# Performer attention and channel mixer on one core: the first channel product of three chunks by Strassen, in a re-ordered list

## Chip, cores and metric

One NeuronCore of a Trainium2 chip runs the whole kernel. The metric is the device time of one execution in microseconds (us). Engines: PE (TensorE, matmuls; weight loads run beside them as PEld), DVE (VectorE), ACT (ScalarE), POOL (GpSimd), SP (SyncE, which here only issues DMAs).

## What is computed

Linear attention with exponential features (8 batches, 8 heads, 576 rows of 64, 128 features), then a mixer over tokens and over channels with weights `w_tok1` 576x256, `w_tok2` 256x576, `w_ch1` 512x1536 and `w_ch2` 1536x512. Inputs and output are float32; the kernel multiplies in float16.

```python
def phi(x):
    proj = np.einsum('bhsd,md->bhsm', x, omega)
    sq = np.sum(x * x, axis=-1, keepdims=True) / 2.0
    h = proj - sq
    return np.exp(h - np.max(h, axis=-1, keepdims=True)) / np.sqrt(m)
kv = np.einsum('bhsm,bhsd->bhmd', k_p, v)
num = np.einsum('bhsm,bhmd->bhsd', q_p, kv)
den = np.einsum('bhsm,bhm->bhs', q_p, k_p.sum(2))[..., None] + 1e-06
x = (num / den).transpose(0, 2, 1, 3).reshape(8, 576, 512)
u = x + (np.maximum(x.transpose(0, 2, 1) @ w_tok1, 0) @ w_tok2).transpose(0, 2, 1)
out = u + np.maximum(u @ w_ch1, 0) @ w_ch2
```

## The kernel before, in words

Rows 0 to 511 of a batch form a chunk (c = 0 to 7, one for each batch). The 64 last rows of all eight batches together form a ninth, the tail chunk (c = 8). For each batch `attention` (L522) makes the features of k and q (matmuls L657, L669; exponentials on ACT, L515), sums them over rows (L681), scales v by the inverse (`vs_`, L687, mostly on POOL), and forms kv (L702, L709) and the normalised output (L735, L737, read by DVE at L744 and L745). `token_mix` (L765) makes the token products (L771, L778, L791), adds x (`uadd`, L794), and has u transposed by a DMA of SP's queue into uT. The tail rows go through L845, L851 and `tail_transpose` (L855).

`channel_mix` (L956) then makes, for one chunk, the first channel product: 12 blocks of 128 hidden channels, each 4 matmuls of 128x512 (L967) into one PSUM bank. A relu on ACT or DVE (L290, L292) reads each bank into r3, in float16. The second channel product (`channel_out_fast`, L858) is already done by Strassen's scheme with 7 products of 2x2 blocks in place of 8: four sums of weight blocks (T, L448, once), four sums of r3 blocks for a chunk, each in two instructions of 128x768 (S and r, L295 by DVE), 7 products of 12 matmuls of 128x256 (L917), in the order X, Y, X, Z, X, Z, X of the banks that they accumulate in, and reads of the banks by DVE (L906) that add u and the parts. The tail chunk does its seven products in halves. Then the rows are stored (L946, L953, L1011). Only chunk 0 does a plain second product (L1001).

Nothing of the order is found at run time. A `Planner` (L121) holds jobs: an engine, the jobs it depends on, the ring slots that it takes and gives back. `ORDER` (L22) is a list of job numbers, kept in the file; each engine issues its own jobs in that order, and a job that waits holds up everything behind it on its engine. A negative number in ORDER is a warm-up matmul in the bank of that number. `SLOT` (L83) says which slot of its ring (or which PSUM bank, 8 in all) each tile gets, and `MOVED` (L93) puts a job on another engine than its usual one.

Of the kernel before, what the change touches and what calls it, by code (L numbers as in the profile page):

```python
# [9 lines left out]
FP32 = mybir.dt.float32  # L10
FP16 = mybir.dt.float16
AF = mybir.ActivationFunctionType
ALU = mybir.AluOpType
# [93 lines left out]
def key_of(name, b):  # L107

    return NEAR.get(str(b), {}).get(name, KEYS[name])


class Job:
    def __init__(self, eng, cost, key, fn, deps, take, give, rows, wire):
# [958 lines left out]
```

## Time and profile before

| | |
|---|---|
| three runs | 282.96, 283.94, 285.21 us |
| median | 283.94 us |
| span of the profiled execution (first to last instruction on the core) | 281.1 us |
| what the median has around that span | 2.84 us |
| mean granted clock of PE while busy, as shares of full speed | 1.00 |
| bytes read from and written to HBM | 35.95 MB, 16.52 MB |

The profiled execution has no time of its own beside its span; the 2.84 us are the difference between the two rows above them. A row of a group of instructions gives line, engine, operation, tiles out and in, shapes and count; then busy us and mean ns of one; then the idle time ahead of them and what ended it. A row of a timeline gives start and length in us, engine, line and tiles; in brackets stands the idle time before it and what released it. A row of the chain gives start, length, engine, what is written, line and count.

### The profile page before, as it was taken

The numbers are of one execution on the slowest core, as the hardware profiler recorded it, in microseconds if no ns is written. First come the engines' busy times: TensorE is split into PE (matmuls) and PEld (weight loads), VectorE is DVE, ScalarE is ACT, GpSimd is POOL, SyncE is SP. The second block draws the span as 40 slices with busy tenths as digits, with TensorE's granted clock in tenths as the row PEclk, the third lists the DMA queues.
The fourth block names the chain that finished last, engine by engine and source line by source line (L and its number), as shares of the span: only waits on it lengthen the run. The fifth ranks groups of instructions, "written<-read, shape, count | busy, mean of one in ns | idle before, by whom it ended". The sixth has DMA issues, their size and how long they took to land.

```text
span 281.1 us, 6278 instructions
## 1 busy us (share of the span) xinstructions
PE 270.3 (96%) x2526; PEld 167.6 (60%) x2526; DVE 222.4 (79%) x462; ACT 138.6 (49%) x288; POOL 92.0 (33%) x116
## 2 busy tenths in 40 slices
PE   6899999999999999999999999999999999999993
PEld 2547546443657755665667647755676467446782
DVE  2589828499999899996997999977995893565992
ACT  1498994049676418743758445734753510031200
POOL 8574994007510872048008710510033000000001
PEclk9999999999999999999999999999999999999999
DMA  6999999999998999997979993960151304030125
GB/s 161 194 189 161 157 169 213 178 191 202 179 218 184 148 172 186 181 198 104 212 178 185 241 135 101 161 156 2 76 97 59 111 0 96 0 149 2 75 90 135
DMA packets 80524, 39.66 MB, mean 141 GB/s; under 512 B 63984, under 2 KB 76016, under 8 KB 80304
## 3 DMA queue, kind: packets, MB, share of 16 engines
q0 software_dynamic: 31744, 17.74, 44.1%
q1 hardware_dynamic: 46832, 15.77, 29.1%
q10 hardware_dynamic: 1920, 5.77, 5.4%
q8 instruction: 19, 0.31, 0.4%
q14 instruction: 9, 0.07, 0.1%
HBM read 35.95 MB, written 16.52 MB: 187 GB/s over the span
## 4 chain that ended last, share of the span: by engine, by line
PE 89%; DVE 3%; DMA 2%; ACT 2%; issue 0%; SPq 0%; DVEq 0%
PE bank L967 32%; PE bank L917 26%; PE bank L791 5%; PE bank L778 5%; PE bank L1001 4%; PE bank L735 3%; PE bank L657 3%; PE bank L702 3%; DMA wc<-in_k_dram 2%; PE bank L669 2%; ACT kp L515 1%; PE bank L845 1%; PE bank L817 1%; PE bank L737 1%; PE bank L771 1%; DVE T L448 1%
## 5 line engine op out<-in xcount | busy, mean ns | idle before, releaser
L967 PE MATMUL bank<-uT,wc 128*128 128x512 f16 x376 | 89.6, 379 | 0.5 <-DVE r L292 0.4
L290 ACT ACTIVATE r<-bank 128x512 f16<-128x512 f32 (+1 forms) x86 | 47.7, 601 | 82.7 <-PE bank L967 61.5
L295 POOL TENSOR_TENSOR vs<-v,vs 128x512 f16<-128x512 f16 x32 | 34.2, 1072 | 94.4 <-DVE vs L683 51.3
L967 PEld LDWEIGHTS <-wc 128*128 128x128 f16 x424 | 38.8, 98 | 38.8 <-issue 1.6
L917 PEld LDWEIGHTS <-r 128*128 128x128 f16 x384 | 36.8, 98 | 8.2 <-issue 1.1
L515 ACT ACTIVATE kp<-bank 128x512 f16<-128x512 f32 x64 | 36.7, 618 | 8.9 <-PE bank L657 7.1
L515 ACT ACTIVATE qp<-bank 128x512 f16<-128x512 f32 x64 | 36.7, 614 | 8.8 <-PE bank L669 5.8
L681 DVE TENSOR_REDUCE km<-kp 128x8 f16<-128x1024 f16 x32 | 38.7, 1208 | 1.2 <-ACT kp L515 1.1
L292 DVE TENSOR_SCALAR r<-bank 128x512 f16<-128x512 f32 (+1 forms) x40 | 26.3, 670 | 15.7 <-PE bank L967 11.3
L745 DVE TENSOR_TENSOR x<-bank,rc 128x320 f16<-128x320 f32 x62 | 30.5, 492 | 2.1
L917 PEld LDWEIGHTS <-S 128*128 128x128 f16 x288 | 28.1, 98 | 5.8 <-issue 0.3
L906 DVE TENSOR_TENSOR o<-u,bank 128x512 f32<-128x512 f16 x28 | 19.0, 679 | 6.2 <-PE bank L917 5.8
L917 PE MATMUL bank<-T,r 128*128 128x256 f16 x192 | 23.8, 273 | 0.0
L917 PE MATMUL bank<-wc,r 128*128 128x256 f16 x192 | 23.6, 273 | 0.0
L917 PE MATMUL bank<-T,S 128*128 128x256 f16 x192 | 23.4, 273 | 0.0
L946 POOL DMA_DIRECT2D out_dram<-o x2 | 1.3, 645 | 61.2 <-issue 61.2
L906 DVE TENSOR_TENSOR o<-o,bank 128x512 f32<-128x512 f32 (+1 forms) x27 | 16.6, 617 | 2.5 <-PE bank L917 1.8
L735 PEld LDWEIGHTS <-qp 128*128 128x128 f16 x256 | 13.5, 98 | 8.1 <-DVE kvsb L286 0.7
L794 DVE TENSOR_TENSOR u<-x,bank 128x512 f16<-128x512 f16 x28 | 17.6, 680 | 0.0
L735 PE MATMUL bank<-kvsb,qp 128*128 128x65 f16 x256 | 15.0, 193 | 0.5 <-DVE kvsb L286 0.5
L791 PE MATMUL bank<-r,w 128*128 128x512 f16 x56 | 14.1, 381 | 0.0
L744 DVE RECIPROCAL rc<-bank 128x5 f32<-128x5 f32 x62 | 11.4, 184 | 2.9 <-PE bank L737 2.2
(119 smaller groups left out, 379.0 us busy)
## 6 DMA issues: line engine op xcount, KB each, us to landing
out_dram<-o ACTq DMA_DIRECT2D x9, 512.0 KB, 2.7
q<-in_q_dram POOLq DMA_DIRECT2D x6, 576.0 KB, 9.7
wc<-in_moe_w_ch_dram POOLq DMA_DIRECT2D x4, 768.0 KB, 9.0
k<-in_k_dram POOLq DMA_DIRECT2D x6, 512.0 KB, 7.8
v<-in_v_dram POOLq DMA_DIRECT2D x6, 512.0 KB, 9.9
out_dram<-o SPq DMA_DIRECT2D x5, 512.0 KB, 3.9
r<-in_q_dram POOLq DMA_DIRECT2D x4, 288.0 KB, 7.5
v<-in_v_dram POOLq DMA_DIRECT2D x4, 256.0 KB, 8.1
```

The lines of the kernel that those rows point to most:

```text
L290: nc.scalar.activation(out=out, in_=in_, func=AF.Relu)
L292: nc.vector.tensor_relu(out=out, in_=in_)
L295: (nc.gpsimd if eng == "POOL" else nc.vector).tensor_tensor(**kw)
L515: nc.scalar.activation(out=out, in_=in_, func=AF.Exp, bias=0.0, scale=1.0)
L681: nc.vector.reduce_max(out=mx, in_=kpv, axis=AX.X)
L735: nc.tensor.matmul(ps[:, k, j * 65 : (j + 1) * 65], st, s[:, i, 0 : D + 1], start=True, stop=True)
L745: nc.vector.tensor_tensor(out=t_x[place("x", b)][:, :, (2 * hp + hs[0]) * D : (2 * hp + hs[0] + n) * D].rearrange("p j (i d) -> p i j d", ...
L791: nc.tensor.matmul(ps, w2_of(tb, j), r1[:, tb, :], start=(tb == 0), stop=(tb == NT - 1))
L794: nc.vector.tensor_tensor(out=t_u[place("u", b)][:, j, :], in0=t_x[place("x", b)][:, j, :], in1=bank(n), op=ALU.add)
L906: nc.vector.tensor_tensor(out=o, in0=a, in1=ps, op=ALU.add)
L917: nc.tensor.matmul(ps[:, j * DH : (j + 1) * DH], a[:, cb, j * P : (j + 1) * P], w[:, cb, :], start=(bank_of(b, j0) not in held and j == j0 ...
L967: nc.tensor.matmul(ps, wc1[:, db, cb * P : (cb + 1) * P], moving(db), start=(db == 0), stop=(db == ND - 1))
```

## The change

Chunks 6, 7 and 8 do the first channel product by Strassen as well (`channel_in_fast`, new). The hidden channels are taken in three groups of 4 blocks (p = 0, 1, 2); each group does 7 products of 4 matmuls of 128x256. Product 1 goes to bank X; X is copied to bank Y (the seed, `go_a`), product 2 adds to Y, and Y is read by a relu (`go_y`). Product 6 adds to X, which is kept in SBUF in float32 (b); product 7 adds again, and X is kept again (c). Product 5 goes to bank Z; c + Z is written to r3 (`go_t`, DVE). Product 3 adds to Z, b + Z is written to r3. Product 4 adds to X, and X is read by a relu (`go_r`). The two blocks written by `go_t` get their relu in place in SBUF (`go_n`), in parts of 4 and 2 hidden blocks.

Four sums of weight blocks of `w_ch1` (`first_weights`, 128x1536 each, all on POOL) are made once. Three of them live in slots of the kT, qT and v rings, the fourth overwrites a block of the weights, and so comes after every plain first product. Four sums of uT (`go_u`, 128x512) are made for each of the three chunks, three of each in those ring slots and the fourth in place, some on POOL and some on DVE.

The sums for the second product are in parts of 4 and 2 blocks for these chunks (3 and 3 before and for the others). Of the 32 sums of chunks 5 to 8, 4 + 4 + 4 + 5 are on POOL now (jobs 841, 845 to 847; 1006 to 1008, 1010; 1167 to 1169, 1172; 1246, 1249 to 1252); before, all were on DVE. For chunks 6 and 7 the second product seeds bank Y by a copy of X as well, on ACT, where DVE read X before.

ORDER, SLOT and MOVED are new. Engine by engine the order of the jobs is that of before up to PE's job 300 (fifth product of chunk 4's second channel product); slots and banks differ from the start. Batch 7's attention comes earlier among the channel products of chunks 4 and 5 than before. The matmuls of the whole program become more (48 of 128x512 go and 84 of 128x256 come for each of the three chunks).

```diff
--- before.py
+++ after.py
@@ ORDER, SLOT, MOVED: new throughout @@
...
+904: "DVE", 951: "POOL", 952: "POOL", 953: "POOL", 954: "POOL", 957: "DVE", 977: "DVE", 979: "DVE", 988: "DVE", 1000: "DVE", 1001: "ACT", 1003: "ACT",
+1006: "POOL", 1007: "POOL", 1008: "POOL", 1010: "POOL", 1054: "DVE", 1066: "DVE", 1105: "DVE", 1117: "DVE", 1118: "DVE", 1122: "DVE", 1125: "DVE",
+1139: "DVE", 1163: "ACT", 1165: "ACT", 1167: "POOL", 1168: "POOL", 1169: "POOL", 1172: "POOL", 1190: "ACT", 1195: "DVE", 1196: "DVE", 1231: "DVE",
+1233: "DVE", 1240: "DVE", 1241: "ACT", 1244: "ACT", 1246: "POOL", 1249: "POOL", 1250: "POOL", 1251: "POOL", 1252: "POOL", 1281: "ACT", 1284: "ACT",
+1285: "ACT", 1286: "SP", 1287: "ACT", 1288: "SP", 1291: "ACT", 1292: "SP",
...
+FAST1 = 6
+def seeded(name):
+
+    return name[0] == "cY" or name[0] == "Y" and len(name) == 2 and name[1] >= FAST1
...
+                    if tag == "bank":
+                        assert self.whole[i] or not seeded(name)
+                        self.whole[i] = covered(name)
...
+    A11, A21, A12, A22 = [wc1[:, 2 * k : 2 * k + 2, e * NH * P : (e + 1) * NH * P] for k in range(2) for e in range(2)]
+    S3 = A21
+    HOME = {1: "kT", 2: "qT", 4: "v"}
+    OF_V = {0: "kT", 1: "qT", 2: "v"}
+
+    def slot_of(tag):
+        t = {"kT": t_kT, "qT": t_qT, "v": t_v}[tag][place(tag, "W")]
+        return t if len(t.shape) == 2 else flat(t)
+
+    def S_of(n):
+        return S3 if n == 3 else slot_of(HOME[n])[:, 0 : 2 * NH * P].rearrange("p (k c) -> p k c", k=2)
+
+    def V_of(n):
+        return slot_of(OF_V[n])[:, 2 * NH * P : 2 * NH * P + 4 * P].rearrange("p (j k s) -> p j k s", j=2, k=2)
+
+    def s_of(c, p, x):
+        i = place("s", (c, p, x))
+        t = flat(t_r1[place("r1", "W")]) if i == 2 else flat(t_x[place("x", "W")])[:, 2 * SM * i : 2 * SM * (i + 1)]
+        return t.bitcast(FP32)
+
+    j_W = {}
+
+    def first_weights(plain):
+        for n, a, b, op in ((1, lambda: A21, lambda: A22, ALU.add), (2, lambda: S_of(1), lambda: A11, ALU.subtract),
+                            (4, lambda: A12, lambda: S_of(2), ALU.subtract), (3, lambda: A11, lambda: A21, ALU.subtract)):
+            e_w = engine("DVE", "POOL")
+            def go_w1(n=n, a=a, b=b, op=op, e_w=e_w):
+                tt(e_w, out=S_of(n), in0=a(), in1=b(), op=op)
+            j_W[n] = add(e_w, 0.95, FAST1 - 0.2, go_w1, deps=[*j_wc1, *([j_W[n // 2]] if n in (2, 4) else [*j_W.values()]), *(plain if n == 3 else [])],
+                         take=[("x", "W"), ("r1", "W")] if n == 3 else [(HOME[n], "W")])
...
-    def channel_out_fast(c, key, jr):
+    def channel_out_fast(c, key, jr, ready=None):
 
         def r3(i, e):
             return t_r3[place("r3", c)][:, NH * e : NH * e + NH, 2 * P * i : 2 * P * i + 2 * P]
         def s_of(i):
             return t_S[:, i - 1]
         sums = {}
-        for g in range(2):
-            part = slice(g * NH // 2, (g + 1) * NH // 2)
-            need = [jr[cb + NH * e] for cb in range(part.start, part.stop) for e in range(2)]
+        PARTS = (slice(0, 3), slice(3, 6)) if ready is None else (slice(0, 4), slice(4, NH))
...
             steps = (
-                (1, lambda: (s_of(1), r3(1, 0), r3(1, 1)), ALU.add),
-                (3, lambda: (r3(1, 0), r3(0, 0), r3(1, 0)), ALU.subtract),
-                (2, lambda: (s_of(2), s_of(1), r3(0, 0)), ALU.subtract),
-                (4, lambda: (s_of(3), r3(0, 1), s_of(2)), ALU.subtract),
+                (1, lambda: (s_of(1), r3(1, 0), r3(1, 1)), ALU.add, [*ready[1, 0][g], *ready[1, 1][g]], ()),
+                (3, lambda: (r3(1, 0), r3(0, 0), r3(1, 0)), ALU.subtract, ready[0, 0][g], (1,)),
+                (2, lambda: (s_of(2), s_of(1), r3(0, 0)), ALU.subtract, ready[0, 0][g], (1,)),
+                (4, lambda: (s_of(3), r3(0, 1), s_of(2)), ALU.subtract, ready[0, 1][g], (2,)),
             )
+            if c < FAST1:
+                steps = tuple((i, what, op, [*ready[0, 0][g], *ready[0, 1][g], *need], after) for i, what, op, need, after in steps)
             prev = []
-            for k, (i, what, op) in enumerate(steps):
-                e_sum = engine("DVE")
-                def go(what=what, op=op, part=part, e_sum=e_sum, c=c, g=g, k=k):
+            for k, (i, what, op, need, after) in enumerate(steps):
+                e_sum = engine("DVE", "POOL")
+                def go_s(what=what, op=op, part=part, e_sum=e_sum, c=c):
                     o, a, b = what()
                     tt(e_sum, out=o[:, part], in0=a[:, part], in1=b[:, part], op=op)
-                job = add(e_sum, 0.5, key + KEYS["S"] + 0.1 * g + 0.01 * k, go, deps=[*need, *prev], take=[("S", c)])
+                job = add(e_sum, 0.5 if c < FAST1 else (0.61, 0.34)[g], key + KEYS["S"] + 0.1 * g + 0.01 * k, go_s,
+                          deps=[*need, *(prev if c < FAST1 else [sums[x][g] for x in after])], take=[("S", c)])
...
+                                             start=(bank_of(b, j0) not in held and j == j0 and cb == 0 and not (seed and k == 1)), stop=False, skip_group_check=True)
...
+                if k == 0 and seed:
+                    e_a = engine("ACT", "DVE")
+                    def go_a(e_a=e_a):
+                        copy(e_a, bank(bank_of("Y", 0)), bank(bank_of("X", 0)))
+                    outs["sA", h] = add(e_a, 0.5, key + KEYS["c2"], go_a, deps=[j], take=[("bank", bank_of("Y", 0))])
+                elif k == 0:
                     outs["sA", h] = read(k, "X", 0, 0, True, [j], False, j0, j1)
                 elif k == 1:
-                    outs["11", h] = read(k, "Y", 0, 0, False, [j, outs["sA", h]], True, j0, j1)
+                    outs["11", h] = read(k, "Y", 0, 0, seed, [j, outs["sA", h]], True, j0, j1)
...
+    def channel_in_fast(c, key, jt):
+
+        def src():
+            return t_uT[place("uT", c)] if c < B else uTt
+        def u_of(k, i):
+            return src()[:, 2 * i : 2 * i + 2, 2 * k : 2 * k + 2, :]
+        v_of = V_of
+        own = [("uT", c)] if c < B else []
+        sums = {}
+        for n, what, op, after in (
+            (1, lambda: (v_of(0), u_of(0, 1), u_of(0, 0)), ALU.subtract, ()),
+            (2, lambda: (v_of(1), u_of(1, 1), v_of(0)), ALU.subtract, (1,)),
+            (4, lambda: (v_of(2), u_of(1, 0), v_of(1)), ALU.subtract, (2,)),
+            (3, lambda: (u_of(0, 1), u_of(1, 1), u_of(0, 1)), ALU.subtract, (1,)),
+        ):
+            e_sum = engine("POOL", "DVE")
+            def go_u(what=what, op=op, e_sum=e_sum):
+                o, a, b = what()
+                tt(e_sum, out=o, in0=a, in1=b, op=op)
+            sums[n] = add(e_sum, 1.0, key - 0.2, go_u, deps=[*jt, *[sums[x] for x in after], *j_W.values()], take=[("V", c)], give=own)
+        ops = {
+            1: ("X", lambda: A11, lambda: u_of(0, 0), [], True), 2: ("Y", lambda: A12, lambda: u_of(1, 0), [], False),
+            6: ("X", lambda: S_of(2), lambda: v_of(1), [sums[2], j_W[2]], False), 5: ("Z", lambda: S_of(1), lambda: v_of(0), [sums[1], j_W[1]], True),
+            7: ("X", lambda: S3, lambda: u_of(0, 1), [sums[3], j_W[3]], False), 3: ("Z", lambda: S_of(4), lambda: u_of(1, 1), [j_W[4]], False),
+            4: ("X", lambda: A22, lambda: v_of(2), [sums[4]], False),
+        }
+        raw = {(i, e): [] for i in range(2) for e in range(2)}
+        for p in range(NH // 2):
+            at = key + 0.15 * p
+            def bank_of(b, p=p):
+                return ("c" + b, c, p)
+            def rows(i, e, p=p):
+                return t_r3[place("r3", c)][:, NH * e + 2 * p : NH * e + 2 * p + 2, 2 * P * i : 2 * P * i + 2 * P]
+            def seen(b, bank_of=bank_of):
+                return bank(bank_of(b)).rearrange("p (t s) -> p t s", t=2)
+            def product(n, deps, give=(), p=p, bank_of=bank_of, at=at):
+                b, a, moving, need, begin = ops[n]
+                def go_p(b=b, a=a, moving=moving, begin=begin):
+                    ps, m, a_ = bank(bank_of(b)), moving(), a()
+                    for t in range(2):
+                        cb = 2 * p + t
+                        for k in range(2):
+                            nc.tensor.matmul(ps[:, 2 * P * t : 2 * P * t + 2 * P], a_[:, k, cb * P : (cb + 1) * P], m[:, :, k, :],
+                                             start=(begin and t == 0 and k == 0), stop=False, skip_group_check=True)
+                j = add("PE", mm(4, 256), at, go_p, deps=[*jt, *j_wc1, *need, *deps], take=[("bank", bank_of(b)), ("r3", c)],
+                        give=[*([("V", c)] if n in (4, 5, 6) else own), *[(x, "W") for x in (*HOME.values(), "x", "r1")], *give])
+                j.heavy = True
+                return j
+            def kept(x, deps, give=(), p=p, seen=seen, at=at):
+                e_k = engine("ACT", "DVE")
+                def go_k():
+                    copy(e_k, s_of(c, p, x).rearrange("p (t s) -> p t s", t=2), seen("X"))
+                return add(e_k, 0.5, at, go_k, deps=deps, take=[("s", (c, p, x))], give=give)
+            def summed(x, b, i, e, deps, free, p=p, seen=seen, rows=rows, at=at, bank_of=bank_of):
+                def go_t():
+                    nc.vector.tensor_tensor(out=rows(i, e), in0=s_of(c, p, x).rearrange("p (t s) -> p t s", t=2), in1=seen(b), op=ALU.add)
+                j = add("DVE", 0.6, at, go_t, deps=deps, give=[("s", (c, p, x))] + ([("bank", bank_of(b))] if free else []))
+                raw[i, e].append(j)
+                return j
+            p1 = product(1, [])
+            e_a = engine("ACT", "DVE")
+            def go_a(e_a=e_a, bank_of=bank_of):
+                copy(e_a, bank(bank_of("Y")), bank(bank_of("X")))
+            ka = add(e_a, 0.5, at, go_a, deps=[p1], take=[("bank", bank_of("Y"))])
+            p2 = product(2, [ka])
+            p5 = product(5, [])
+            e_y = engine("ACT", "DVE")
+            def go_y(e_y=e_y, rows=rows, seen=seen):
+                relu_to(e_y, rows(0, 0), seen("Y"))
+            raw[0, 0].append(add(e_y, 0.5, at, go_y, deps=[p2], give=[("bank", bank_of("Y"))]))
+            p6 = product(6, [ka])
+            kb = kept("b", [p6])
+            p7 = product(7, [kb])
+            kc = kept("c", [p7])
+            t22 = summed("c", "Z", 1, 1, [kc, p5], False)
+            p3 = product(3, [t22])
+            summed("b", "Z", 1, 0, [kb, p3], True)
+            p4 = product(4, [kc])
+            e_r = engine("ACT", "DVE")
+            def go_r(e_r=e_r, rows=rows, seen=seen):
+                relu_to(e_r, rows(0, 1), seen("X"))
+            raw[0, 1].append(add(e_r, 0.5, at, go_r, deps=[p4], give=[("bank", bank_of("X"))]))
+        ready = {k: [raw[k][:2], raw[k][2:]] for k in ((0, 0), (0, 1))}
+        for i, e in ((1, 1), (1, 0)):
+            ready[i, e] = []
+            for g, part in enumerate((slice(0, 4), slice(4, NH))):
+                e_p = engine("DVE", "ACT")
+                def go_n(part=part, i=i, e=e, e_p=e_p):
+                    x = t_r3[place("r3", c)][:, NH * e + part.start : NH * e + part.stop, 2 * P * i : 2 * P * i + 2 * P]
+                    relu_to(e_p, x, x)
+                ready[i, e].append([add(e_p, (0.33, 0.2)[g], key + 0.4, go_n, deps=raw[i, e][2 * g : 2 * g + 2])])
+        return ready
     def channel_mix(c, key, jt):
+        if c == FAST1:
+            first_weights(plain)
+        if c >= FAST1:
+            channel_out_fast(c, key, [], channel_in_fast(c, key, jt))
+            return
         def moving(db):
...
```

More of the change, by code (lines that the diff above doesn't have):

```diff
@@ L92 @@
+    "05213631112301500014136304021232114651231623742351410060014270252060340526300741202712053433260126021035304223045011127214514032453103105422"
+    "11003415726201014751312631412573070114025010620511240705041203116002107314500536754103022754106112057403122507122151273130403011024102721132"
+    "00412612730207540262711523341625021741520173036415126423720504130026432102356741320411103040603025011000132022101122712100416735010362241113"
+    "7006043570012171020101471300142104"
 )
 MOVED = {
-    42: "DVE", 43: "ACT", 45: "ACT", 48: "DVE", 51: "ACT", 53: "ACT", 56: "ACT", 60: "ACT", 62: "ACT", 65:
@@ new lines @@
+"DVE", 141: "DVE", 145: "ACT", 147: "DVE", 163: "ACT", 169: "DVE", 171: "ACT", 175: "DVE", 179: "ACT", 190: "ACT", 194: "ACT", 228: "ACT", 242: "DVE",
+256: "DVE", 265: "DVE", 278: "DVE", 280: "DVE", 286: "DVE", 300: "DVE", 324: "ACT", 399: "DVE", 426: "DVE", 428: "DVE", 432: "DVE", 434: "DVE", 484:
+"DVE", 498: "DVE", 552: "DVE", 556: "DVE", 562: "DVE", 593: "ACT", 594: "ACT", 634: "DVE", 662: "DVE", 690: "DVE", 692: "DVE", 700: "DVE", 702: "DVE",
+727: "ACT", 728: "ACT", 768: "DVE", 796: "DVE", 830: "DVE", 834: "DVE", 841: "POOL", 845: "POOL", 846: "POOL", 847: "POOL", 863: "ACT", 864: "ACT",
@@ L109, in key_of, with __init__, covered @@
     return NEAR.get(str(b), {}).get(name, KEYS[name])
+class Job:
+    def __init__(self, eng, cost, key, fn, deps, take, give, rows, wire):
+        self.eng, self.cost, self.key, self.fn = eng, cost, key, fn
+        self.deps, self.take, self.give = deps, take, give
+        self.rows, self.wire = rows, wire
+        self.end = None
+        self.heavy = False
+FAST1 = 6
+def covered(name):
+    kind = name[0][0] if isinstance(name[0], tuple) else name[0]
+    if kind in ("X", "Y", "Z"):
+        return len(name) == 2
+    return kind in ("h2", "h3", "h4", "qp", "htt", "cX", "cY", "cZ") or kind == "h1" and name[1] > 0
+def seeded(name):
+    return name[0] == "cY" or name[0] == "Y" and len(name) == 2 and name[1] >= FAST1
 class Job:
@@ L128, in __init__ @@
         self.held = {}
+        self.whole = [False] * places["bank"]
     def add(self, eng, cost, key, fn, deps=(), take=(), give=(), rows=False, wire=0.0):
@@ L145, in run @@
                 self.warm(-1 - n)
+                self.whole[-1 - n] = True
                 continue
@@ L161, in place, with engine @@
         return self.held[tag, name]
-    def engine(self, usual):
+    def engine(self, usual, *others):
         return MOVED.get(len(self.jobs), usual)
@@ L716, in attention @@
                        give=[("kp", (b, hp)), ("vs", (b, hp)), ("kpt", b)] + ([("vbd", b)] if dma_in else []))
-            e_kv = engine("ACT" if b >= NPE or BY[("ko", "ko1")[b]][hp] == "A" else "DVE")
+            e_kv = engine(*("ACT", "DVE") if b >= NPE or BY[("ko", "ko1")[b]][hp] == "A" else ("DVE", "ACT"))
             def kv_out(hp=hp, n_kv=n_kv, e_kv=e_kv):
@@ L883, in channel_out_fast @@
         ops = (
-            ("X", lambda: r3(0, 0), W11, []),
-            ("Y", lambda: r3(0, 1), W21, []),
+            ("X", lambda: r3(0, 0), W11, sum(ready[0, 0], [])),
+            ("Y", lambda: r3(0, 1), W21, sum(ready[0, 1], [])),
             ("X", lambda: s_of(2), T2, sums[2]),
@@ L889, in channel_out_fast @@
             ("Z", lambda: s_of(3), W22, sums[4]),
-            ("X", lambda: r3(1, 1), T4, sums[1]),
+            ("X", lambda: r3(1, 1), T4, [*sums[1], *sum(ready[1, 1], [])]),
         )
@@ L896, in channel_out_fast @@
         tail = c == B
+        seed = c >= FAST1 and not tail
+        of_s = (2, 3, 4, 5, 6)
         def bank_of(b, j0):
@@ L917, in go @@
                             nc.tensor.matmul(ps[:, j * DH : (j + 1) * DH], a[:, cb, j * P : (j + 1) * P], w[:, cb, :],
-                                             start=(bank_of(b, j0) not in held and j == j0 and cb == 0), stop=False, skip_group_check=True)
+                                             start=(bank_of(b, j0) not in held and j == j0 and cb == 0 and not (seed and k == 1)), stop=False, skip_group_check=True)
                     held[bank_of(b, j0)] = True
-                deps = [*need, *jr, *j_T, *j_wc2] + [outs[x, h] for x in ({2: ["sA"], 4: ["s2"], 5: ["22"], 6: ["s3"]}.get(k, []))]
-                j = add("PE", mm((j1 - j0) * NH, DH), key + KEYS["c2"] + step * k, go, deps=deps, take=[("bank", bank_of(b, j0))], give=[("r3", c)] + ([("S", c)] if need else []))
+                deps = [*need, *(jr if c < FAST1 else []), *j_T, *j_wc2] + [outs[x, h] for x in ({1: ["sA"] if seed else [], 2: ["sA"], 4: ["s2"], 5: ["22"], 6: ["s3"]}.get(k, []))]
+                j = add("PE", mm((j1 - j0) * NH, DH), key + KEYS["c2"] + step * k, go, deps=deps, take=[("bank", bank_of(b, j0))], give=[("r3", c)] + ([("S", c)] if k in of_s else []))
                 j.heavy = True
-                if k == 0:
+                if k == 0 and seed:
[4 more added lines that the diff above has]
+                elif k == 0:
                     outs["sA", h] = read(k, "X", 0, 0, True, [j], False, j0, j1)
                 elif k == 1:
-                    outs["11", h] = read(k, "Y", 0, 0, False, [j, outs["sA", h]], True, j0, j1)
+                    outs["11", h] = read(k, "Y", 0, 0, seed, [j, outs["sA", h]], True, j0, j1)
                 elif k == 2:
```

27 lines of the change are left out of this document (9 added, 18 removed), and 105 rows, old and new, of the table ORDER.

## Prediction

> **What bounds the kernel now.** I read the page's busy shares and slices first, then the chain that ended last.
>
> ```profile
> span 281.1 us, 6278 instructions
> PE 270.3 (96%) x2526; PEld 167.6 (60%) x2526; DVE 222.4 (79%) x462; ACT 138.6 (49%) x288; POOL 92.0 (33%) x116
> POOL 8574994007510872048008710510033000000001
> PE 89%; DVE 3%; DMA 2%; ACT 2%; issue 0%; SPq 0%; DVEq 0%
> ```
>
> TensorE (PE) is busy for 96% of the span and carries 89% of the chain, so a matmul saved is time saved while PE never has to wait. DVE at 79% is the second load. POOL, in slices of 7 us, does almost nothing in the last quarter. The lists of both kernels agree on every engine up to PE's job 300, which begins here at 180.38 us; from there all is in a new order. So I read busy time by stage, split there:
>
> ```profile
> 40.00:180.38 140.38, 139.97 (x1323) 85.19 (x1321) 122.90 (x251) 80.26 (x165) 52.27 (x64) 1.00 1.07 180
> 180.38:276.27 95.89, 95.60 (x777) 62.52 (x775) 72.80 (x148) 29.75 (x59) 9.33 (x10) 1.00 0.26 71
> 276.27:281.10 4.83, 0.00 (x0) 0.00 (x0) 0.42 (x1) 0.00 (x0) 0.00 (x0) 0.88 0.55 148
> ```
>
> The columns are the stretch, its length, busy PE, weight loads, DVE, ACT, POOL, then the granted clock. In the last third PE works 95.60 of 95.89 us: there is 0.3 us of idle to win and everything to lose. DVE has 72.80 of 95.89, POOL 9.33, and 4.83 us follow the last matmul. The chain in that stretch, in order of time (start, length, engine, line, count):
>
> ```profile
> 179.52 0.86 PE bank L967 x4
> 180.38 1.31 PE bank L917 x12
> 238.88 13.81 PE bank L967 x64
> 265.73 10.52 PE bank L917 x96
> 276.27 0.42 DVE o L906
> ```
>
> L967 is the first channel product in 128x512 matmuls: 13.81/64 = 216 ns each. L917 is the second one, already by Strassen in 128x256: 1.31/12 = 109.2 ns each (10.52/96 = 109.6).
>
> **The change part by part.**
>
> *PE.* For each of batch 6, batch 7 and the tail chunk, 48 matmuls at 216 ns (10.36 us) go and 84 of 128x256 come. These are of L917's shape, so 84 x 109.2 = 9.17 us: -1.19 us a chunk, **-3.57 us** for three. The weight load must hide:
>
> ```profile
> L917 PEld LDWEIGHTS <-r 128*128 128x128 f16 x384 | 36.8, 98 | 8.2 <-issue 1.1
> L290 ACT ACTIVATE r<-bank 128x512 f16<-128x512 f32 x84 | 46.9, 606 | 82.5 <-PE bank L967 61.5 <-PE bank L778 11.4 <-DVE o L906 5.4
> L292 DVE TENSOR_SCALAR r<-bank 128x512 f16<-128x512 f32 x38 | 25.5, 684 | 15.2 <-PE bank L967 11.3 <-PE bank L778 3.6
> L906 DVE TENSOR_TENSOR o<-u,bank 128x512 f32<-128x512 f16 x28 | 19.0, 679 | 6.2 <-PE bank L917 5.8
> L295 DVE TENSOR_TENSOR S<-r 128x768 f16<-128x768 f16 x16 | 8.8, 551 | 0.6 <-ACT r L290 0.4
> L295 POOL TENSOR_TENSOR vs<-v,vs 128x512 f16<-128x512 f16 x32 | 34.2, 1072 | 94.4 <-DVE vs L683 51.3 <-PE bank L669 22.2 <-PE bank L917 13.8
> L295 POOL TENSOR_TENSOR T<-vt,mask 128x1024 f16<-128x1024 f16 x1 | 1.9, 1904 | 0.0
> ```
>
> A load of 98 ns fits under 109, as it does in L917 today. If it did not, the three chunks would cost 84 x (216 - 109.2) = 9 us each more; nothing in L917's rows points there.
>
> *Reads of PSUM.* A chunk had 12 relus (606 ns on ACT, 684 on DVE). Now each of three groups has a seed copy, two relus, two kept copies and two sums: 15 reads by ACT or DVE and 6 sums on DVE, at about 0.60 to 0.68 us (the L290, L292 and L906 rows). That is 21 x 0.65 = 13.7 us for 12 x 0.64 = 7.7. Beside this come four relus in place (1024 or 512 elements) and four sums of uT (512), about 0.5 us each on DVE by the 551 ns of its 768-element sum. Three chunks bring some 30 us to ACT and DVE, which in this stretch have 66 and 23 us free. By total they hide behind PE; by order they may not, because every group is a chain: product, copy, product, sum, product. I added up the PE work that the list puts between producer and consumer against one read each. The cover is above zero nearly everywhere, but -0.2 us at the second group-1 product of chunk 6, and 0.0 to 0.2 at four others (a token product of batch 7, two products of the tail chunk, the tail's last products). With ring waits (a sum on POOL ahead of a kv product, banks of qp) I walk to 1.4 us in the first 28 us and 0.9 after: **+2.3 us** for the thin list. Bounds: 0, when all covers hold, to 4.
>
> *POOL.* This part decides. All four weight sums (128x1536) go to POOL, 17 sums for the second product (4 of 768, 7 of 1024, 6 of 512 elements), and 7 of uT's (512). POOL's price is 1072 ns for 512 elements and 1904 for 1024, so 1.7 ns an element: 2.8 us for 1536 and 1.5 for 768 (estimates from these rows). That is 11.1 + 25.7 + 7.5 = 44 us of new work for an engine that did 9.3 in this stretch. In the kernel before no sum for the second product ever ran beside POOL there: its last rows are
>
> ```profile
> 208.87 1.05 POOL L295 TENSOR_TENSOR vbd<-vt,vbd 128x512 f16<-128x512 f16 x1 [1.22 <-DVE vbd L594]
> 210.35 3.08 POOL L295 TENSOR_TENSOR vs<-v,vs 128x512 f16<-128x512 f16 x3 [0.43 <-DVE vs L683]
> 274.64 1.28 POOL L946 DMA_DIRECT2D out_dram<-o  x2 [61.21 <-issue]
> ```
>
> What happens when both engines sum in SBUF is seen earlier, in the timelines of DVE and POOL (start, length):
>
> ```profile
> 20.62 0.83 DVE L631 COPY qpt<-qpt 128x512 f16<-128x512 f16 x1 [0.49 <-ACT qpt L515]
> 63.08 1.21 DVE L681 TENSOR_REDUCE km<-kp 128x8 f16<-128x1024 f16 x1
> 64.51 0.91 DVE L448 TENSOR_TENSOR T<-wc,T 128x1536 f16<-128x1536 f16 x1
> 65.33 1.81 DVE L448 TENSOR_TENSOR T<-wc 128x1536 f16<-128x1536 f16 x1
> 71.13 1.82 DVE L448 TENSOR_TENSOR T<-wc,T 128x1536 f16<-128x1536 f16 x1
> ```
>
> ```profile
> 20.22 1.07 POOL L295 TENSOR_TENSOR vs<-v,vs 128x512 f16<-128x512 f16 x1
> 63.28 1.05 POOL L295 TENSOR_TENSOR vbd<-vt,vbd 128x512 f16<-128x512 f16 x1 [16.52 <-DVE vbd L594]
> 64.85 1.48 POOL L295 TENSOR_TENSOR vs<-v,vs 128x512 f16<-128x512 f16 x1
> 71.05 1.07 POOL L295 TENSOR_TENSOR vs<-v,vs 128x512 f16<-128x512 f16 x1
> ```
>
> A DVE sum alone takes 0.91 us. POOL's at 64.85 found it running and took 1.48 in place of 1.05; the next DVE sum started under POOL's, which ended at 66.33, and ended 0.81 us after that. At 71.13 DVE started 0.08 us behind POOL, and ended 0.83 us after POOL's end at 72.12. So the two take turns, whole instructions at a time. The copy from SBUF to SBUF at 20.62 started under POOL's sum (20.22 to 21.29) and ended at 21.45, 0.16 us behind it, so I count relus in place like sums. The reduction at 63.08 lost nothing (1.21) beside POOL. The Trainium skill, page "SBUF — State Buffer", section "Who interferes with whom", has a rule that speaks against this change: a DVE sum of two SBUF inputs, and a copy or scalar operation in a two-port mode, exclude a GpSimd instruction that reads SBUF, and whichever issues second waits out the other; a reduction does not contend. The rows of sums agree; no row here shows a relu in place, and if only the sums counted, place B below would fall to about 1.5 us and the forecast from 288.0 to 287.1, while by the rule it stays at 288.0.
>
> Reads of PSUM with one SBUF operand or none are not slowed themselves, but they queue on DVE behind a sum that waits. So I laid the new POOL instructions beside DVE's list at PE's positions without stalls. Three places have PE behind them:
> - A, near 206 us: the third weight sum (POOL, 2.8 us) ahead of a sum of chunk 5 (DVE) that product 3 (X) of chunk 5's second product needs. Price 2.2 us if POOL starts first, 0 if DVE does; they are 0.6 us apart. I take half: **1.1**.
> - B, 230 to 240 us: three POOL sums of 1.9 us for chunk 6 in a row, against in-place relus and two DVE sums; behind these on DVE wait the kept sums of chunk 7's groups 2, 1 and 0, and product 3 of chunk 6 waits for one. Price 2 to 4 us on PE; 3 as walked.
> - C, 249 to 273 us: POOL sums of chunk 7 against uT's second sum and the last DVE sum ahead of the tail chunk's group 2 (1.15 and 1.5 us); then POOL sums of the tail chunk against two DVE sums that its last X products need (0.8 twice). Together 4.2 as walked.
> Lower bound for all three 0, upper 10. For B and C I take six tenths of 7.2, because each counts only where POOL happens to start first: **4.3 us**.
>
> *The rest, at nothing.* Slots and banks given anew: before 180.38 only they differ, and from 40 us on PE idles 0.41 us there, so ±0.5. Transposed loads on SP's queue are issued later, but hold at least 1.2 us of slack by the list (kT of batch 7, the tightest, about 1 us); if one were late PE would wait for what is missing. The SP stores behind them and the one store left on POOL at the tail, now behind its sums, still come before DVE's last reads, so the 4.83 us after the last matmul stay.
>
> *Sum.* The profiled execution has a span of 281.1; the three runs are 282.96, 283.94 and 285.21, so the median stands 2.84 above this span, and I sum against 281.1 + 2.84 = 283.94. -3.57 + 2.3 + 1.1 + 4.3 = +4.1: **288.0 us**.
>
> **The rivals.**
> 1. *The lists work as written: faster.* Mechanism: at B and C the POOL sum always ends before DVE's turn, because ACT's relus feed both early enough. For it: PE's 95.60 of 95.89 us now shows what such a list can do, and the uses in the list lie several products off. Against: the rows at 65.33 and 71.13, where as careful a list still collided. It decides from where collisions cost below 0.7 us on PE in all: 283.94 - 3.57 + 0 to 0.7 = 280.4 to 281.1.
> 2. *Collisions fall into slack, thin chains do not.* The gain is eaten by the 2.3 us and some of A: 283.94 - 3.57 + 2.3 + 0 to 1.8 = 282.7 to 284.5. Also here: half the collisions, up to 286.
> 3. *All of A, B, C as walked, each late one making the next later.* -3.57 + 2.3 + 2.2 + 3 + 4.2 = +8.1: 292.0.
> 4. *Strassen saves nothing on PE,* because a load with another weight tile each 109 ns is exposed. L917 speaks against it; 283.94 + 2.3 or more, so it falls in with the forecast's range.
>
> **How the numbers follow.** About 1% (2.8 us) is what a measurement of this kernel can tell from no change. Rival 1 gets 0.2, rival 2 0.27 and the forecast with rivals 3 and 4 0.53 (of these 3 and 4 together 0.1). Faster by over 1%, below 281.1: 0.2. Within 1%, 281.1 to 286.8: 0.27. Slower, above: 0.53. The likeliest case alone runs from 286.8 to 291.5. Since cases of both signs hold much of the chance, the range goes from the full PE gain, 280.4, to 291.5 just below rival 3.
>
> **What would show it.** Right: PE busy falls by about 3.6 us; PE idle between 205 and 273 us grows from 0.3 to some 7, its waits ending on DVE sums or copies; DVE sums of S (551 ns now) averaging over 0.8 us wherever POOL sums run, each ending some half microsecond after POOL's end; PE waits at chunk 5's third product and among chunk 7's groups. Wrong: PE idle below 3 us in the last third with DVE's sums at 551 ns, or PE gaps that end on ACT or on a DMA; matmuls of the new product above 115 ns; a difference before 180 us.

## The result, and the profile after

| | before | after |
|---|---|---|
| median (4 runs each) | 284.44 us | 295.19 us |
| lowest to highest | 282.96 to 285.21 | 294.72 to 297.14 |
| span of the profiled execution | 281.1 us | 292.9 us |

The ratio is 1.040 (95% interval 1.034 to 1.045): the change costs 10.75 us, where 4.1 were forecast. The changed kernel's page, with its groups of the chain:

```profile
span 292.9 us, 6580 instructions
PE 271.6 (93%) x2634; PEld 179.6 (61%) x2634; DVE 238.7 (81%) x466; ACT 153.3 (52%) x312; POOL 140.7 (48%) x142
POOL 8574993027403770182059104877950373291450
PE 74%; DVE 14%; ACT 4%; issue 3%; DMA 3%; POOL 0%; ACTq 0%; DVEq 0%; POOLq 0%
```

PE's share of the chain falls from 89% to 74%, and DVE's rises from 3% to 14%. POOL's busy time grows by 48.7 us, nearly all at the end. The stages of the last third (columns as before: length, busy PE, weight loads, DVE, ACT, POOL, granted clock):

```profile
180.38:203.00 22.62, 21.45 (x219) 11.98 (x217) 18.65 (x38) 17.76 (x40) 18.55 (x11) 1.00 0.27 61
203.00:213.00 10.00, 9.69 (x127) 8.46 (x125) 9.68 (x25) 1.16 (x3) 8.59 (x6) 1.00 0.50 97
213.00:233.00 20.00, 20.00 (x166) 15.58 (x164) 15.90 (x29) 9.32 (x16) 5.60 (x5) 1.00 0.32 91
233.00:247.00 14.00, 9.67 (x80) 7.71 (x79) 13.56 (x17) 4.89 (x9) 7.66 (x4) 0.96 0.20 29
254.00:267.00 13.00, 10.63 (x97) 9.14 (x95) 11.07 (x13) 5.74 (x11) 10.07 (x6) 1.00 0.21 82
274.00:283.30 9.30, 7.34 (x66) 6.04 (x64) 8.73 (x13) 2.01 (x4) 6.88 (x5) 1.00 0.28 115
```

PE idles most in three stretches: 4.3 us at 233 to 247, 2.4 at 254 to 267 and 2.0 at 274 to 283.3, where POOL is busy for 55 to 77% of the time. POOL's share alone does not make the loss: from 180 to 213 us it is busier still (82 and 86%), and PE idles 1.5 us in all. Between 213 and 233 us, the channel product of chunk 6 runs without a stall, though POOL works there too. The worst place, 233 to 247, first PE, then DVE, then POOL, each from its own timeline of the changed kernel:

```profile
240.38 0.60 PE L970 MATMUL bank<-T,S 128*128 128x256 f16 x4
242.09 1.05 PE L970 MATMUL bank<-T,S 128*128 128x256 f16 x8 [1.11 <-DVE S L311]
244.94 0.60 PE L1058 MATMUL bank<-kT 128*128 128x256 f16 x4 [1.80 <-DVE r L1071]
246.28 1.01 PE L1058 MATMUL bank<-uT,v 128*128 128x256 f16 x4 [0.74 <-DVE r L1071]
```

```profile
238.06 1.72 DVE L308 TENSOR_SCALAR r<-r 128x512 f16<-128x512 f16 x1
239.70 2.34 DVE L311 TENSOR_TENSOR S<-S,r 128x512 f16<-128x512 f16 x1
242.07 2.22 DVE L311 TENSOR_TENSOR S<-r,S 128x512 f16<-128x512 f16 x1
244.22 0.67 DVE L1071 TENSOR_TENSOR r<-x,bank 128x512 f16<-128x512 f32 x1
```

```profile
237.51 2.12 POOL L311 TENSOR_TENSOR S<-S,r 128x1024 f16<-128x1024 f16 x1 [0.90 <-DVE S L311]
239.59 2.16 POOL L311 TENSOR_TENSOR r<-r 128x1024 f16<-128x1024 f16 x1
241.72 2.29 POOL L311 TENSOR_TENSOR S<-r,S 128x1024 f16<-128x1024 f16 x1
```

Read DVE against POOL. The relu in place at 238.06 ends at 239.78, just after POOL's first sum (239.63). The next DVE sum ends at 242.04, 0.29 us after POOL's second (241.75); the third at 244.29, 0.28 after POOL's third (244.01). Three short instructions became 6.2 us, and the read of PSUM at 244.22, which the product at 244.94 needs, stood behind them.

Stalls below are measured from one matmul's start to the next, less its own length. They come out longer than the idle time shown, because the last matmul's modelled end (0.60 for four of 109 ns) counts as busy.

| place | stall, us | what PE waited for |
|---|---|---|
| 182 | 0.45 | a POOL sum for batch 6's kv |
| 195 to 196 | 1.20 | batch 7's normalised output, behind DVE's L641 |
| 204 | 0.63 | DVE, late behind a POOL sum that it needs |
| 234 to 236 | 1.00 | a DVE read of PSUM (0.23), then a seed copy (0.77) |
| 240.8 to 246.3 (B) | 4.15 | a DVE sum of S, then two kept sums |
| 258, 265 (C) | 2.70 | uT's second sum; a kept sum behind an S sum |
| 277 to 283 (C, tail) | 2.45 | the last S sums |

That is 12.6 us. Beside it the clock, in two windows of the changed kernel:

```profile
246.00:249.40 3.40, 3.12 (x15) 2.23 (x15) 1.52 (x3) 1.64 (x2) 0.00 (x0) 0.50 0.00 0
249.40:252.00 2.60, 2.60 (x26) 2.33 (x24) 1.81 (x3) 0.00 (x0) 0.00 (x0) 1.00 0.00 0
```

Right behind place B the granted clock is 0.50 for 3.4 us: another 1.7 us. So 12.6 + 1.7 - 3.6 (PE's saving) = 10.7 us by the chain, against 10.75 in the medians. The spans of the two traces lie 11.8 apart, because the one after is late from the start. These are rows of the chains of before, of a second trace of the kernel before, and of after, at the same eight matmuls of the token product:

```profile
170.07 1.73 PE bank L791 x8
```

```profile
171.09 1.73 PE bank L791 x8
```

```profile
171.29 1.73 PE bank L838 x8
```

The kernel before differs from itself by 1.0 us there. In the traces of e1 to e6 and e12 below, whose list and slots up to there are those of the changed kernel, the same matmuls begin between 171.15 and 175.27 us. So the start of the program varies by more than 1.2 us, and nothing in the 1.2 has to be the new slots and banks. From these rows to the end of the span it is 111.0 us before and 121.6 after: 10.6 more.

### The profile page after: what moved, and what is told of

Read it like the earlier page. It is cut to its first block, busy times and chain, and to the rows that moved or that the text cites. A ratio compares the mean times of both kernels' runs of the same rounds, so it can differ in the third digit from the quotient of the medians.

```text
span 292.9 us, 6580 instructions
## 1 busy us (share of the span) xinstructions
PE 271.6 (93%) x2634; PEld 179.6 (61%) x2634; DVE 238.7 (81%) x466; ACT 153.3 (52%) x312; POOL 140.7 (48%) x142
## 4 chain that ended last, share of the span: by engine, by line
PE 74%; DVE 14%; ACT 4%; issue 3%; DMA 3%; POOL 0%; ACTq 0%; DVEq 0%; POOLq 0%
PE bank L970 20%; PE bank L1125 19%; PE bank L1058 7%; PE bank L825 4%; PE bank L838 4%; PE bank L1160 4%; DVE S L311 3%; DMA wc<-in_k_dram 3%; PE bank L749 2%; PE bank L704 2%; PE bank L782 2%; PE bank L716 2%; DVE r L308 2%; DVE km L728 2%; DVE o L959 1%
## 5 line engine op out<-in xcount | busy, mean ns | idle before, releaser
L311 POOL TENSOR_TENSOR vs<-v,vs 128x512 f16<-128x512 f16 x31 | 33.1, 1072 | 74.0 <-DVE vs L730 51.1
L1125 PE MATMUL bank<-uT,wc 128*128 128x512 f16 x280 | 67.8, 379 | 0.1
L306 ACT ACTIVATE r<-bank 128x512 f16<-128x512 f32 (+1 forms) x78 | 44.1, 603 | 43.2 <-PE bank L1125 26.4
L970 PE MATMUL bank<-T,r 128*128 128x256 f16 x192 | 24.5, 278 | 0.4 <-DVE o L959 0.4
L308 DVE TENSOR_SCALAR r<-bank 128x512 f16<-128x512 f32 (+1 forms) x30 | 19.8, 665 | 6.2 <-PE bank L825 4.8
L959 DVE TENSOR_TENSOR o<-o,bank 128x512 f32<-128x512 f32 (+1 forms) x25 | 15.3, 615 | 2.8 <-PE bank L970 2.2
L311 POOL TENSOR_TENSOR S<-r 128x768 f16<-128x768 f16 (+2 forms) x4 | 7.0, 1752 | 20.8 <-ACT r L306 19.5
L302 ACT COPY x<-bank 128x512 f32<-128x512 f32 x10 | 5.8, 586 | 19.8 <-PE bank L1058 10.0
L311 POOL TENSOR_TENSOR vbd<-vt,vbd 128x512 f16<-128x512 f16 x6 | 6.3, 1052 | 19.5 <-DVE vbd L641 16.5
```

Source lines behind the costliest of these rows:

```text
L306: nc.scalar.activation(out=out, in_=in_, func=AF.Relu)
L308: nc.vector.tensor_relu(out=out, in_=in_)
L311: (nc.gpsimd if eng == "POOL" else nc.vector).tensor_tensor(**kw)
L959: nc.vector.tensor_tensor(out=o, in0=a, in1=ps, op=ALU.add)
L970: nc.tensor.matmul(ps[:, j * DH : (j + 1) * DH], a[:, cb, j * P : (j + 1) * P], w[:, cb, :], start=(bank_of(b, j0) not in held and j == j0 ...
L1125: nc.tensor.matmul(ps, wc1[:, db, cb * P : (cb + 1) * P], moving(db), start=(db == 0), stop=(db == ND - 1))
```

## The experiments

The theory: DVE and POOL take turns for instructions that read two operands from SBUF or copy within it, and what queues on DVE behind a waiting one holds PE. The rival: the new chain of product, copy, product, sum is too tight for PE by itself. A second rival: POOL merely delivers late.

**All new POOL sums on DVE** (e1), only those for the second product (e2). Edits in `MOVED`:

```diff
-841: "POOL", ... 951: "POOL", ... 1252: "POOL"
+841: "DVE", ... 951: "DVE", 955: "DVE", ... 1252: "DVE"
```

> The changed kernel with all 28 new sums of POOL (4 of weights, 17 for the second product, 7 of uT) on DVE, at the same places of the list. Turn-taking theory (DVE's sums wait out POOL's, and what queues behind them on DVE holds PE): the waits behind POOL go; DVE gets about 17 us more work in the last third, of which some 2 to 4 us show, so 284 to 288 us, and no DVE sum above its own length. Rival, thin list (the chains product, copy, product, sum of the new channel product stall PE by themselves): 292 us or more, since DVE only gets fuller.

> The changed kernel with only the 17 sums for the second product on DVE; weight sums and uT sums stay on POOL. Turn-taking theory: the stalls at 240 to 246 us and in the tail go (some 8 us with the lost clock), those at 195 us (weight sums beside batch 7's attention, 1.2 us) and a part of those at 257 us stay: 286 to 289 us. Rival, thin list: 292 us or more.

e1: 287.9 us, ratio 1.015 (1.009 to 1.022), 7.3 below the changed kernel although DVE has more to do (its busy time is 237.7 us, 12 above that of e4 below, where these sums are not on DVE and its own hardly wait). e2: 291.3, ratio 1.024 (1.018 to 1.030), higher than expected. In its trace the weight sums, still on POOL, now make batch 7's `vs` on DVE late (a PE stall of 1.9 us at 204.5) and the places at 195, 257 and 277 us stay. e1 speaks against the thin list, which wants 292 or more; e2 lies just under that and doesn't decide.

**POOL's sums cut to a stub** (e3), and **POOL busy but not reading** (e4):

```diff
+    def tt_new(eng, out, in0, in1, op):
+        if eng == "POOL":                                   # e3
+            out, in0, in1 = [x[..., 0:16] for x in (out, in0, in1)]
+        tt(eng, out=out, in0=in0, in1=in1, op=op)
...
+        if eng == "POOL":                                   # e4
+            tt(eng, out=out[..., 0:2], in0=in0[..., 0:2], in1=in1[..., 0:2], op=op)
+            nc.gpsimd.memset(out, 0.0)
+            nc.gpsimd.memset(out, 0.0)
```

> The changed kernel with the 28 new sums of POOL cut to 16 columns of each row block (the rest of each sum is left out), so that list, engines and waits stay and POOL's instructions take about 0.2 us. Turn-taking or slow POOL: 282 to 285 us, that is the PE saving of 3.6 us less about 1 us in the head and 1 to 2 us of thin chains. Rival, thin list: 291 us or more, nothing changes for it.

> The changed kernel with each of the 28 new sums of POOL replaced by a sum of two columns (which keeps its waits) and two fills of the whole output, which write SBUF but read none of it; the sums' values are left out. POOL stays busy nearly as long. If it is the turn-taking of instructions that read SBUF: DVE's sums keep their own length, and the time is 284 to 288 us. If it is only that POOL delivers late: the stalls stay as they are and the time is 292 us or more. A fill that also excludes DVE would show as DVE sums of 1.5 to 2.5 us beside the fills.

e3: 282.9 us, ratio 0.995 (0.992 to 0.999). e4: 283.2 us, ratio 0.996 (0.993 to 0.998), a little below the 284 to 288 expected. e4 decides. Its DVE and POOL at the same place as above:

```profile
235.27 0.68 DVE L311 TENSOR_TENSOR S<-r 128x1024 f16<-128x1024 f16 x1
236.59 0.81 DVE L308 TENSOR_SCALAR r<-r 128x512 f16<-128x512 f16 x1
237.32 0.41 DVE L311 TENSOR_TENSOR S<-S,r 128x512 f16<-128x512 f16 x1
237.76 0.42 DVE L311 TENSOR_TENSOR S<-r,S 128x512 f16<-128x512 f16 x1
238.10 0.68 DVE L1079 TENSOR_TENSOR r<-x,bank 128x512 f16<-128x512 f32 x1
```

```profile
236.30 0.95 POOL L316 MEMSET S<- 128x1024 f16 x1
237.31 0.98 POOL L317 MEMSET S<- 128x1024 f16 x1
238.25 0.20 POOL L311 TENSOR_TENSOR r<-r 128x8 f16<-128x8 f16 x1
238.51 0.95 POOL L316 MEMSET r<- 128x1024 f16 x1
```

The two sums that took 2.34 and 2.22 us take 0.41 and 0.42, under POOL's fill of 237.31 to 238.29. POOL is as busy as in the changed kernel (58.5 us in the last third against 58.3), its results come nearly as late, and 12 us are gone. DVE's busy time, for the same 466 instructions, falls from 238.7 to 225.5 us: 13 us of the changed kernel's were waiting. So it is neither POOL's slowness nor the thin list. What these two cost is left in this trace: stalls of 0.45, 0.23 and 0.77 us by the list, together 1.45 (e3 has the same), and one of 0.59 at 272 us that waits for POOL's fills.

**Place by place**: only chunk 6's four POOL sums on DVE (e5), only the weight sums (e6), only chunk 7's and the tail chunk's thirteen (e12), all in `MOVED`.

> The changed kernel with only the four POOL sums for chunk 6's second product on DVE, all else as it was. If each place pays for its own collisions, the stalls between 236 and 246 us (4.9 us, and the 1.7 us of half clock behind them) shrink to about 1 us and the others stay: 290 to 292 us. If the stalls only move on to the next place: 294 us or more.

> The changed kernel with only the four weight sums on DVE. If they cost by holding back batch 7's attention (stalls at 195 and 196 us, 1.2 us): 293 to 294 us. If they are a main part of the loss: below 292 us. If DVE, which is then 4 us fuller between 185 and 212 us, delays that attention itself: 295 us or more.

> The changed kernel with chunk 7's and the tail chunk's thirteen new POOL sums (nine for the second product, four of uT) on DVE; chunk 6's and chunk 5's and the weight sums stay on POOL. If each place pays for its own collisions: the stalls at 258, 265 and 277 to 283 us (5.2 us) shrink to 1 to 2 us and those at 236 to 246 us stay: 290 to 292.5 us. If DVE, fuller by about 7 us of sums, pays the same: 294 us or more.

e5: 290.8 us, ratio 1.025 (1.018 to 1.032), 4.4 below the changed kernel: the 4.15 of stall at B and the half clock behind it are gone from its trace, and the stalls of C stay (4.85 against 5.15). e12: 291.7, ratio 1.026 (1.022 to 1.030), 3.5 below: the stall at 258 falls from 1.42 to 0.28 and that at 265 goes; 1.3 at 277 stay, and B's stay whole (4.2 against 4.15). e6: 294.9, ratio 1.039 (1.033 to 1.045), no gain: the stalls at 195 shrink, but new ones of 0.4 at 190 and 193 and 0.8 at 210 come from the fuller DVE. So B and C pay nearly independently. These medians of four carry the spread of the program's start; from the eight matmuls shown above (175.27 us in e5, 171.15 in e12) to the end of the span, e5's trace is 5.0 us and e12's 2.9 us shorter than the changed kernel's.

**The kernel before once more** (e7), and **idle POOL work beside it** (e10 sums, e11 fills):

```diff
+    beside = sb([P, 640], FP16, "beside")
+    for c, (job, need) in first_sums.items():
+        at = ORDER.index(plan.jobs.index(job))
+        for i in range(3):
+            ORDER.insert(at, len(plan.jobs))
+            add("POOL", 2.0, 0.0, lambda: nc.gpsimd.tensor_tensor(out=beside, in0=flat(wc2)[:, 0:640], in1=flat(wc2)[:, 640:1280], op=ALU.add), deps=need)
```

> The kernel before once more, for the first 180 us alone, where both kernels have the same list: if the changed kernel's delay of 1.2 to 1.4 us there is the spread of the first loads, this trace should be as late as that of the changed one in places; if it is slots and banks, it should lie near the first trace of before. Time as before, 282 to 286 us.

> The kernel before, with three idle POOL sums of 128x640 from SBUF (1.35 us each, nobody waits for them) added where the sums for the second product of chunks 4 to 7 begin on DVE. Nothing else changes. Turn-taking theory: each DVE sum there waits for a POOL sum, some 3 to 4 us of delay a chunk, of which PE sees 1 to 2: 287 to 292 us, with DVE sums of 1.2 to 1.9 us. Rival, that the loss in the changed kernel comes from Strassen's chains and not from POOL: as before, 283 to 286 us.

> As the kernel with idle POOL sums, with each sum replaced by two fills of the same 128x640, which write SBUF and read none of it, of about the same length. Turn-taking of instructions that read SBUF: 283 to 286 us and DVE sums of 0.55 us. If any POOL work beside DVE costs: as slow as the kernel with sums.

e7 is shown above: 284.26 us, and 1.0 us late at 171 us. e10: 285.4 us, ratio 1.006 (1.003 to 1.008), short of the 287 to 292 of its theory; e11: 284.8, ratio 1.002 (0.999 to 1.005). The difference between the medians is too small to tell. At chunks 5 to 7 the idle sums of e10 ran too early to meet DVE's: chunk 5's were through at 192.4 us and DVE's sums there began at 198.0, and those of chunks 6 and 7 were through at 225.8, 1.1 us before DVE's sums of the usual 0.55 us. A place in the list fixes the order on one engine, not the time against another. At chunk 4 they did meet. POOL, DVE and PE of e10 there:

```profile
166.52 4.73 POOL L1050 TENSOR_TENSOR beside<-wc 128x640 f16<-128x640 f16 x3
169.06 0.93 DVE L295 TENSOR_TENSOR S<-r 128x768 f16<-128x768 f16 x1
169.92 1.75 DVE L295 TENSOR_TENSOR r<-r 128x768 f16<-128x768 f16 x1
174.78 1.47 PE L921 MATMUL bank<-T,S 128*128 128x256 f16 x12 [0.92 <-DVE o L910]
```

The same two DVE sums of e11, beside fills:

```profile
165.29 4.07 POOL L1050 MEMSET beside<- 128x640 f16 x6
168.59 0.56 DVE L295 TENSOR_TENSOR S<-r 128x768 f16<-128x768 f16 x1
169.07 0.55 DVE L295 TENSOR_TENSOR r<-r 128x768 f16<-128x768 f16 x1
```

Beside sums that nobody waits for, DVE's two take 0.93 and 1.75 us, the second ending 0.42 us after POOL's last; beside fills they take 0.56 and 0.55. PE then idles 0.92 us behind DVE in e10, and not at all there in e11. So the turn-taking and its price to PE show in the kernel before as well, without the new chains.

**The same work in another list** (e8, e9). Engines and places of the jobs from about 170 us on were searched anew, over the jobs' dependences with the lengths of these traces and the rule that a reading POOL sum and a DVE sum or relu in place exclude each other. `ORDER`, `SLOT` and `MOVED` are new; the computation is unchanged.

> The same work as the changed kernel, with engines and places of the jobs from about 170 us on chosen anew so that a sum on POOL and a sum or a relu in place on DVE seldom want to run at once (62 jobs change engine, most of them between ACT and DVE). Turn-taking theory: nearly the whole PE saving shows, 279 to 283 us. Rival, that 44 us of new work on POOL and DVE can't be fitted in: 286 us or more.

> As the kernel that chose engines and places anew, now also keeping 8 us between the issue of a transposed load of uT and its first use (7.1 us were measured there, with a 2.2 us stall of PE and 3.4 us of half clock behind it) and the order of the stores at the end (7 in a row on ACT's queue there, so that 7.3 us followed the last read in place of 4.4). 61 jobs change engine. Turn-taking theory: 280 to 283 us, below the kernel before. Rival, that the new work can't be fitted in: 286 us or more.

e8: 288.5 us, ratio 1.016 (1.010 to 1.022), a miss: no stall behind POOL was left, but the search had moved uT's transposed load to 5.1 us ahead of the moment at which PE had nothing else to do (203.39 to 208.47), and the load took longer. The load in e8's chain, PE's timeline, and the windows ahead of and behind the stall:

```profile
203.39 7.10 DMA uT<-u
```

```profile
210.54 0.61 PE L1041 MATMUL bank<-uT,wc 128*128 128x256 f16 x4 [2.07 <-DMA uT<-u]
```

```profile
208.00:211.10 3.10, 1.03 (x13) 0.69 (x11) 2.70 (x7) 0.00 (x0) 0.00 (x0) 1.00 0.85 71
211.10:214.50 3.40, 3.40 (x22) 2.32 (x19) 2.95 (x6) 0.57 (x1) 0.05 (x1) 0.50 0.00 0
```

That is 2.2 us of stall and 1.7 of half clock; seven stores in a row on ACT's queue left 7.3 us behind the start of the last read where before has 4.8, 2.5 more. e9, with both kept apart: 281.32 us against 284.05, ratio 0.991 (0.987 to 0.994). It beats the kernel before and the changed one. Its page and windows:

```profile
PE 268.8 (96%) x2634; PEld 178.4 (64%) x2634; DVE 228.9 (82%) x475; ACT 149.0 (53%) x306; POOL 134.2 (48%) x139
```

```profile
203.00:233.00 30.00, 30.00 (x299) 24.72 (x296) 25.82 (x53) 10.30 (x20) 15.92 (x11) 1.00 0.36 82
233.00:247.00 14.00, 14.00 (x131) 12.54 (x129) 10.51 (x20) 5.95 (x11) 5.46 (x4) 1.00 0.12 37
247.00:274.50 27.50, 27.50 (x252) 24.37 (x250) 23.34 (x46) 6.50 (x12) 12.35 (x9) 1.00 0.24 88
```

PE is never idle from 203 us to the end of its matmuls, with POOL still at 134.2 us in all (140.7 in the changed kernel). One DVE sum of the last third is still caught, at 199.9 us (1.09 us in place of 0.55). POOL need not be given up; its sums only have to run where DVE reads PSUM.

## Why the prediction was wrong

The way was right, the size was not: +10.75 where +4.1 was forecast. 295.19 us lies above the range of 280.4 to 291.5, and above the 292.0 that was the worst case worked out.

- **PE's saving**, -3.57: right. The new matmuls run at 109 ns like the old ones. From the eight matmuls shown above (174.23 us in e3) to the end of the span, e3 takes 108.8 us and the kernel before 111.0; without the stalls in each (1.45 and 0.3) that is 3.3 less.
- **The thin list**, +2.3: 1.45 as e3 and e4 show it alone.
- **Place A**, +1.1: 0. DVE's sum came 0.06 us ahead of the weight sum (209.21 against 209.27); POOL waited (3.45 us in place of 3.1), and nobody waited for POOL. With 0.06 us between them that was luck.
- **Places B and C**, +4.3. This step failed: "For B and C I take six tenths of 7.2, because each counts only where POOL happens to start first." Every one counted, and 9.3 us came of it (4.15, 2.70, 2.45): 5.0 more than the term, of which the discount is 2.9 and prices walked too low are 2.1. The discount took the starts for independent. They are not: POOL's sums stand back to back, so the DVE instruction that gets its turn is followed by the next POOL sum, which has already waited, and DVE's next one meets that. In the rows above three of DVE's in a row paid. Single sums were longer too: 2.12 for 1024 elements where 1.90 was taken, 3.09 for 1536 (2.8).
- **Not in the sum:** place 195 us (1.2). The weight sums before it (POOL, 3.1 us each) held back a DVE product of 8 elements in batch 7's attention. POOL and DVE in the changed kernel:

```profile
191.96 3.10 POOL L311 TENSOR_TENSOR v<-wc,qT 128x1536 f16<-128x1536 f16 x1
```

```profile
193.48 1.63 DVE L641 TENSOR_TENSOR vbd<-rct,mask 128x8 f16<-128x8 f16 x1
```

  It takes 0.19 us in e4. I had looked only at large sums. Place 204 (0.6) is missing too: there DVE waited for a POOL sum that it needs. So is the half clock behind a stall (1.7), which no row of before could show, because PE hardly idled there.
- **The difference**, 6.6 us: 5.0 at B and C, 1.2 and 0.6 at 195 and 204, 1.7 of clock, less 1.1 at A and 0.85 of the list, is 6.5.
- **The signs.** PE's idle time between 205 and 273 us came to 6.7 us (some 7 forecast), and DVE's sums were long and ended with POOL's. But PE's busy time rose from 270.3 to 271.6, with 1.7 of half clock in it, where a fall by 3.6 was to show, and chunk 5's third product had no wait.
- **Rival 1** is not what this list did; e9's list, at 281.32, came within 0.3 us of its 280.4 to 281.1. **Rival 2** fails: none of the collisions at B and C fell into slack. **Rival 3** was nearest. **Rival 4** is refuted by the 109 ns.

The rule cited there, the Trainium skill's "SBUF — State Buffer", section "Who interferes with whom", agrees with these runs in all that they test: sums of two SBUF inputs against reading POOL sums wait whole instructions, and against fills, which only write, they don't. The relu in place, which no row of before showed, does wait, 1.72 us in the changed kernel, as that section says of operations in a two-port mode.

Left open: why e1 stays at 287.9. Its stalls (1.4 us at 209, 0.9 at 237, 1.3 at 273) all end on a full DVE, but no run took them apart.

## What to carry to other kernels

Before moving an elementwise sum from DVE to POOL to relieve DVE, lay both queues side by side in time: a POOL sum that reads SBUF stops each DVE instruction that reads two SBUF operands, or copies within SBUF, for its whole length, however small that one is, and every read of PSUM queued behind it. Put such POOL work where DVE reads PSUM, and count back-to-back POOL sums as a sequence of collisions, not as independent chances. In a kernel that PE bounds, add the half clock that can follow a stall of some 2 us (1.7 us lost, both in the changed kernel and in e8).

## What the runs showed of the hardware

- A fill on POOL doesn't hold up a DVE sum (0.41 us under a fill of 0.98), but it did hold up the relu in place: 0.81 us at 236.59 in e4, ending 0.15 us after the fill, against 0.29 alone.
- After a single idle of 2.1 us (e8) PE's granted clock was 0.50 for 3.4 us. The Trainium skill, page "TensorE: Matmul & The Clock Gate", section "What's actually happening", has the clock fall after an idle window of about 3.4 us. Here the clock fell although PE had worked for a third of the 3.1 us ahead of it, so PE need not be wholly idle for that long. The stalls of 1.42 and 1.28 us at place C brought no such fall.
- A transposed load of uT took 7.1 us (e8), with a 512 KB store issued at the same time and another transposed load issued 4 us later. All others in the traces of this case took 4.2 to 6.0 us. Which of the two made it late is open.
